# Tokens stationary in the second layer, weights split by bit operations, exponentials slot by slot for the first pairs

## The chip, the cores and the metric

The kernel runs on one core of a Trainium2 chip. It has five engines with a queue each: TensorE (matmuls; PE in the profile, PEld for its weight loads), VectorE (DVE), ScalarE (ACT), GpSimd (POOL) and SyncE (SP), which issues most transfers. An engine takes its instructions in order. The metric is device time in microseconds, the median of three runs.

## The reference

Eight batches of local attention feed a feed-forward block with a gate. All tensors are float32; the block's three weights are drawn as float64 and enter with 64 bits.

```python
# B, H, S, D = 8, 8, 576, 64; d_model 512, d_ff 1024
scores = q @ k.T / sqrt(D)
mask_plain = (rel >= 0) & (rel < 32)                       # heads 0 to 3
mask_dil = (rel >= 0) & (rel < 128) & (rel % 4 == 0)       # heads 4 to 7
attn = exp(scores - max); attn = attn / (sum(attn) + 1e-9)
x = (attn @ v), heads joined: (B, S, 512)
h = maximum(x @ w_in, 0)                                   # (B, S, 1024)
conv_out = conv_w[0]*h[s-1] + conv_w[1]*h[s] + conv_w[2]*h[s+1]
out = (h / (1 + exp(-conv_out))) @ w_out                   # (B, S, 512)
```

## The kernel before

**Precision.** Matmuls of the two layers take a cheap 32-bit type (`F32R`). Each operand is split into a rounded part and its remainder (`a` and `b`, or index 0 and 1), and a product is three matmuls (`TERMS`): part by part, part by remainder, remainder by part.

**Attention.** Heads go in pairs; a batch has pairs 0 and 1 (plain) and 2 and 3 (dilated). A pair's 576 queries lie in nine slots of 64 keys for 128 partitions. Its steps: 76 to 80 small matmuls of scores into the PSUM tile `att` (L248), mask added by VectorE (L254, L257), largest value of each slot (L260), subtraction (L262), exponential on ScalarE (L264), sum (L266), 1e-9 added (L268), reciprocal (L270), product (L271), transpose (L273), 96 small matmuls with the values into `att` (L283). ScalarE copies the result to `x` rounded (L320); the remainder is a subtraction on VectorE (L335), or, in batches 0 and 1, matmuls with minus the unit matrix on TensorE (L327, L330) and a second pair of ScalarE copies (L333). There is one `att`, so scores and values of all pairs take turns in it.

**First layer.** 128 hidden features (a chunk, eight of them) by 288 tokens (a half) are twelve matmuls (L353) into a PSUM tile `mm`, or `nn` for every second chunk of batch 0; there are two of each. ReLU goes to `h` on ScalarE (L360). `h` has three buffers, each with a whole chunk. Gating of a chunk: middle tap on ScalarE (L371), two taps on VectorE (L365), sigmoid (L376), product with `h` on VectorE (L378), which frees `h`; rounded part `g` on ScalarE (L380), remainder on VectorE (L382). `c`, the working tile, has three buffers, `g` one set of eight chunks.

**Second layer.** 128 output features by 288 tokens are 24 matmuls (L395): a 128x128 piece of `wo` is stationary and `g` moves. ScalarE copies out of PSUM (L402); a store goes out feature by feature, and the host turns the result.

**Weights.** A chunk of 512 words per partition comes in 64-bit form, two 32-bit words a value. ScalarE (L428) and VectorE (L430 to L441) build the rounded float32 and the rest. For the first ten of sixteen chunks TensorE adds them and takes off the rounded part (L450 to L452: a float32 matmul and two of `F32R`, 512 columns each), and ScalarE copies the remainder (L455). For six chunks VectorE does it (L457, L463).

**Order.** Every step is a task with an engine, a cost, a due time and buffers. `Planner.order` plays them through; on each engine, of the tasks that could start soon, the one with the earliest due time is taken. So the due times set the order, which is fixed when the program is built.

## Time and profile before

| | us |
|---|---|
| median of three runs (549.78 to 550.69) | 549.82 |
| span of the profiled execution, first to last instruction | 549.1 |
| TensorE busy | 522.4 |
| VectorE busy | 415.7 |
| ScalarE busy | 298.1 |
| mean granted TensorE clock, of full speed | 0.990 |

The profiled execution's span is 0.7 us below the median of the runs; the rest lies around it. "Busy" counts overlapping instructions once. A window row gives its length, then for an engine its busy time and, in brackets, instructions. Chain rows give start, length, engine, tile and line. Group rows give line, engine, operation, output<-input with shapes and count, then busy time and mean ns, then idle time ahead and what ended it.

### The profile page before, as it was taken

To read this page: it belongs to the slowest core of one execution; us is meant where nothing else is said; L and a number is where in the kernel's file an instruction comes from. 1 tells how busy PE (TensorE), PEld (TensorE's weight loads), DVE (VectorE), ACT (ScalarE), POOL (GpSimd) and SP (SyncE) were. 2 spreads that over 40 slices of the span, in tenths; PEclk is the share of its full clock that TensorE was granted. 3 is DMA by queue.
4 is the path that set the end of the run, shared out by engine and by line. 5 is a ranking of instruction groups with operands and counts; after the bars stand their busy time and mean duration, and the time that the engine had idled before them with its cause. 6 is when DMAs were issued, how large, how long until landed. Compare 5 with 4: busy or idle time off the path is not lost.

```text
span 549.1 us, 19084 instructions
## 1 busy us (share of the span) xinstructions
PE 522.4 (95%) x8664; PEld 497.2 (91%) x8664; DVE 415.7 (76%) x695; ACT 298.1 (54%) x556; POOL 0.9 (0%) x12
## 2 busy tenths in 40 slices
PE   3499978999999999999999999999999999999997
PEld 2468876999999999999999999999989999999997
DVE  4968998899997389946998389946988389946920
ACT  2457784855752486337742486237742486337721
POOL 0000000000000000000000000000000000000000
PEclk9999996999999999999999999999999999999999
DMA  7756513331044102630055102530045102300011
GB/s 247 268 157 215 195 52 137 119 121 44 7 138 152 30 23 65 200 110 23 13 161 170 32 23 72 190 113 23 17 152 162 45 23 58 117 26 23 0 44 44
DMA packets 17072, 52.31 MB, mean 95 GB/s; under 512 B 2016, under 2 KB 3168, under 8 KB 16992
## 3 DMA queue, kind: packets, MB, share of 16 engines
...
q10 hardware_dynamic: 144, 0.08, 0.1%
q14 instruction: 12, 0.10, 0.1%
...
## 4 chain that ended last, share of the span: by engine, by line
PE 92%; DVE 3%; ACT 2%; DMA 2%; issue 1%; ACTq 0%
PE nn L395 38%; PE mm L353 35%; PE att L283 8%; PE att L248 6%; PE nn L450 2%; PE nn L353 2%; PE att L327 1%; DMA qk<-in_qk_d_dram 1%; DMA qk<-in_qk_p_dram 1%; PE nn L451 0%; PE nn L452 0%; DVE pt L273 0%; DVE s L271 0%; PE att L330 0%; DVE c L365 0%
## 5 line engine op out<-in xcount | busy, mean ns | idle before, releaser
L365 DVE SCALAR_TENSOR_TENSOR c<-h,conv_sb,c 128x576 f32<-128x576 f32 x128 | 103.9, 815 | 48.4 <-ACT c L371 46.9
L360 ACT ACTIVATE h<-mm 128x288 f32<-128x288 f32 x120 | 48.8, 408 | 50.4 <-PE mm L353 50.1
L402 ACT COPY out<-nn 128x288 f32<-128x288 f32 x64 | 25.5, 400 | 70.1 <-PE nn L395 66.1
L378 DVE TENSOR_TENSOR c<-c,h 128x576 f32<-128x576 f32 x64 | 47.6, 755 | 9.4 <-ACT c L376 7.8
L283 PEld LDWEIGHTS att<-pt,v 32*64 32x64 f32 x3072 | 40.8, 138 | 14.8 <-DVE s L257 4.6
L283 PE MATMUL att<-pt,v 32*64 32x64 f32 (+2 forms) x3072 | 44.2, 232 | 9.4 <-DVE s L257 3.5
L371 ACT ACTIVATE c<-h,conv_sb 128x576 f32<-128x576 f32 x64 | 49.7, 776 | 1.3
L248 PE MATMUL att<-qk 64*32 64x64 f32 x2432 | 36.2, 235 | 11.0 <-DMA qk<-in_qk_d_dram 5.5
L248 PEld LDWEIGHTS att<-qk 64*32 64x32 f32 x2432 | 30.2, 111 | 16.9 <-DMA qk<-in_qk_d_dram 5.5
L376 ACT ACTIVATE c<-c 128x576 f32<-128x576 f32 x64 | 42.5, 678 | 2.1 <-DVE c L365 1.6
L353 PE MATMUL mm<-x2a,wi 128*128 128x288 f32 x144 | 40.5, 296 | 0.0
L353 PE MATMUL mm<-x1a,wi 128*128 128x288 f32 x144 | 40.3, 296 | 0.0
L353 PE MATMUL mm<-x3a,wi 128*128 128x288 f32 x144 | 40.3, 295 | 0.0
L353 PE MATMUL mm<-x0a,wi 128*128 128x288 f32 x144 | 40.3, 295 | 0.0
L395 PE MATMUL nn<-g2a,wo 128*128 128x288 f32 x128 | 37.0, 304 | 0.0
L395 PE MATMUL nn<-g0a,wo 128*128 128x288 f32 x128 | 36.4, 299 | 0.2
L395 PE MATMUL nn<-g6a,wo 128*128 128x288 f32 x128 | 36.6, 299 | 0.0
L395 PE MATMUL nn<-g3a,wo 128*128 128x288 f32 x128 | 36.4, 299 | 0.0
L395 PE MATMUL nn<-g1a,wo 128*128 128x288 f32 x128 | 36.4, 299 | 0.0
L395 PE MATMUL nn<-g4a,wo 128*128 128x288 f32 x128 | 36.4, 299 | 0.0
L395 PE MATMUL nn<-g5a,wo 128*128 128x288 f32 x128 | 36.4, 299 | 0.0
L395 PE MATMUL nn<-g7a,wo 128*128 128x288 f32 x128 | 36.1, 300 | 0.1
...
## 6 DMA issues: line engine op xcount, KB each, us to landing
...
out_dram<-out SPq DMA_DIRECT2D x28, 288.0 KB, 2.2
...
out<-in_w_in_dram SPq DMA_DIRECT2D x8, 512.0 KB, 4.5
out<-in_w_out_dram SPq DMA_DIRECT2D x8, 512.0 KB, 4.2
out_dram<-out SPq DMA_DIRECT2D x8, 144.0 KB, 1.8
```

Of the source, the lines that this page charges most:

```text
L248: nc.tensor.matmul(sc.t[quad * 32:quad * 32 + 32, slot // 4, slot % 4 * W:slot % 4 * W + W], q, k, start=i == 0, stop=i == len(parts) - 1, ...
L283: nc.tensor.matmul(tv.t[hd * 64:hd * 64 + 64, bank, o:o + n], v.t[quad * 32:quad * 32 + 32, block // 2, block % 2 * 64:block % 2 * 64 + 64 ...
L327: nc.tensor.matmul(tv.t[:, t, 0:128], minus, main[:, t], start=False, stop=True, skip_group_check=True)
L353: nc.tensor.matmul(ps.t[:, 0:HALF], wi[jw][fc][:, k * 128:k * 128 + 128], x[k].t[jx][:, hf * HALF:hf * HALF + HALF], start=(k == 0 and i = ...
L360: relu.append(plan.add("ACT", 0.4, due + 1.6 * u + 1.6, lambda fc=fc, hf=hf, ps=ps: nc.scalar.activation(out=h[fc].t[:, 1 + hf * HALF:1 + ...
L365: nc.vector.scalar_tensor_tensor(out=c[fc].t, in0=h[fc].t[:, k:S + k], scalar=conv_sb[:, k, fc:fc + 1], in1=c[fc].t, op0=ALU.mult, op1=ALU ...
L371: t = plan.add("ACT", 0.777, d, lambda fc=fc: nc.scalar.activation(out=c[fc].t, in_=h[fc].t[:, 1:S + 1], func=AF.Copy, scale=conv_sb[:, 1, ...
L376: t = plan.add("ACT", 0.686, d + 1.0, lambda fc=fc: nc.scalar.activation(out=c[fc].t, in_=c[fc].t, func=AF.Sigmoid), [t], [c[fc]], "sigmoid")
L378: t = plan.add("DVE", 0.755, d + 1.5, lambda fc=fc: nc.vector.tensor_tensor(out=c[fc].t, in0=c[fc].t, in1=h[fc].t[:, 1:S + 1], op=ALU.mult ...
L395: nc.tensor.matmul(ps.t[:, 0:HALF], wo[jw][2 * dm + k // 4][:, k % 4 * 128:k % 4 * 128 + 128], g[k].t[jg][:, hf * HALF:hf * HALF + HALF], ...
L402: outs.append(plan.add("ACT", 0.4, out_due + 3.3 + 3.3 * u, lambda hf=hf, ps=ps, o=o: nc.scalar.copy(out=o.t[:, hf * HALF:hf * HALF + HALF ...
L450: nc.tensor.matmul(ps.t, ident, t(), start=True, stop=False)
```

## The change

1. **Second layer.** Tokens become stationary (128 columns of `g`) and `wo` moves with 512 output features: 24 matmuls a job (L431) and one copy of 128x512 (L441). Batch 0 does two halves of 256 instead, since the halves of `wo` come one after the other. The output is stored token by token, and the host does not turn it.
2. **`g` for two batches.** 576 tokens are four and a half times 128. A `g` tile now holds two chunks, both parts, and 640 tokens: an even batch writes columns 0 to 575, the odd batch after it 64 to 639. An even batch does four jobs from column 64; the odd one five, the first with 64 tokens of each batch. A chunk of the odd batch is written when the even batch's jobs have read it (`done`).
3. **Weights.** Two chunks of 512 are converted together (1024 words), eight times. The rounded part is now cut by a mask in the second step (0x3ffff000), and the remainder is put together from the low word by a shift, a shift with an or, a mask and one product (L504 to L510). Nothing of it is on TensorE, and the ten sums are gone. The 24 convolution weights have their own short path (`few_weights`).
4. **Softmax.** For the first eight pairs (`SLOTS`: batches 0 and 1) ScalarE does nine exponentials, one a slot, with the negated largest value as bias and the sum as second output (L279); VectorE does no subtraction and no sum, and ScalarE scales the bias and adds the 1e-9 (L275, L283). The other pairs have a 65th column with 1e-9 in `s` that the sum takes in.
5. **Dilated copies.** `x` is written in order and `att` read in steps, where before read in order and wrote in steps.
6. **Order.** The due times are a new table, `DUE`, one for each task or series of tasks; `out` has two buffers instead of three.

```diff
+GW = S + 64
+PAIRED = 1024
+SLOTS, HELPED = 0xff, 0xff
+DUE = {
+    "first": (72.60, 66.90, 228.40, 589.20, 119.60, 531.50, -87.70, 234.00),
...
-    slots("s", 3, [128, 9, W])
+    ss = slots("s", 3, [128, 9, W + 1])
-    slots("g", NF, [128, S], F32R, 2)
+    slots("g", NF // 2, [128, 2, 2, GW], F32R)
-    slots("out", 3, [128, 1024])
-    slots("w", 2, [128, 512], F32, 2)
-    slots("r", 2, [128, 512], F32R)
+    slots("out", 2, [128, DM])
+    slots("raw", 2, [128, 2 * PAIRED], I32)
+    slots("t", 1, [128, PAIRED])
...
+        last = plan.add("DVE", 0.755, soft + 0.5, lambda: nc.vector.tensor_reduce(
+            out=m.t, in_=flat(), axis=AX.X, op=ALU.max, negate=slotwise), [last], [s, m])
+        if slotwise:
+            last = plan.add("ACT", 0.23, soft + 1.0, lambda: nc.scalar.mul(out=m.t, in_=m.t, mul=SCALE), [last], [m])
+            def exps():
+                for i in range(9):
+                    nc.scalar.activation(out=s.t[:, i, 0:W], in_=s.t[:, i, 0:W], func=AF.Exp, bias=m.t[:, i:i + 1],
+                                         scale=SCALE, accum_out=z.t[:, i:i + 1])
+            last = plan.add("ACT", 2.7, soft + 1.5, exps, [last], [s, m, z], "exp")
+            last = plan.add("ACT", 0.23, soft + 2.1, lambda: nc.scalar.add(out=z.t, in_=z.t, add=1e-9), [last], [z])
...
+            hi = plan.add("ACT", 0.675, d + 2.0, lambda fc=fc: nc.scalar.copy(out=half(fc, 0), in_=c[fc].t),
+                          [t, *(done[fc] if odd else [])], [c[fc], g[fc // 2]])
...
+        begins = [64 + 64 * odd + 128 * j for j in range(4)]
+        if odd:
+            begins = [0] + begins
+        jobs = [(c0, hf) for hf in range(2) for c0 in begins] if b == 0 else [(c0, None) for c0 in begins]
...
+                    nc.tensor.matmul(ps.t[:, 0:n], g[k // 2].t[:, k % 2, jg, c0:c0 + 128],
+                                     w.rearrange("p h c -> p (h c)") if hf is None else w[:, hf],
+                                     start=(k == 0 and i == 0), stop=(k == NF - 1 and i == 2))
...
+        last = plan.add("ACT", 1.14, due, lambda: nc.scalar.activation(out=t(), in_=hw(), func=AF.Abs), [load], [raw, tb])
+        last = step(0.69, [last], lambda: nc.vector.tensor_scalar(
+            out=t(), in0=t(), scalar1=2.0 ** -15, scalar2=None, op0=ALU.max))
+        last = step(0.69, [last], lambda: nc.vector.tensor_scalar(
+            out=bits(t), in0=bits(t), scalar1=3, scalar2=0x3ffff000,
+            op0=ALU.logical_shift_left, op1=ALU.bitwise_and))
+        top = step(1.22, [last], lambda: nc.vector.scalar_tensor_tensor(
+            out=bits(t), in0=bits(hw), scalar=-0x40000000, in1=bits(t), op0=ALU.bitwise_and, op1=ALU.bitwise_or))
+        high = plan.add("ACT", 1.14, due, lambda: nc.scalar.copy(out=hi, in_=shaped(t(), hi)), [top], [tb])
+        left = step(0.69, [load], lambda: nc.vector.tensor_scalar(
+            out=bits(lw), in0=bits(lw), scalar1=9, scalar2=None, op0=ALU.logical_shift_right))
+        left = step(1.22, [left], lambda: nc.vector.scalar_tensor_tensor(
+            out=bits(lw), in0=bits(hw), scalar=23, in1=bits(lw), op0=ALU.logical_shift_left, op1=ALU.bitwise_or))
+        last = step(0.69, [top, left], lambda: nc.vector.tensor_scalar(
+            out=bits(hw), in0=bits(t), scalar1=-0x800000, scalar2=None, op0=ALU.bitwise_and))
+        return [high, plan.add("DVE", 1.22, due, lambda: nc.vector.scalar_tensor_tensor(
+            out=lo, in0=shaped(lw().bitcast(U32), lo), scalar=2.0 ** -43, in1=shaped(hw(), lo),
+            op0=ALU.mult, op1=ALU.mult), [last], [raw])]
```

`lw` and `hw` are the low and high words of a value, every second word of `raw`.

Three places in the order of the built programs. Numbers behind an underscore tell buffers apart; `pt` is the transposed tile, `v` the values.

TensorE, near the start, before: a correction, the second value block, then the first weight sum.

```order
L327 MATMUL att_159<-x0a,minus 128x128 x4
L330 MATMUL att_159<-x0a,minus 128x32 x2
L283 MATMUL att_159<-pt_113,v_101 64x32 x8
L283 MATMUL att_159<-pt_113,v_101 64x64 x24
L283 MATMUL att_159<-pt_113,v_101 64x32 x16
L450 MATMUL nn_162<-w0b,ident 128x512
L451 MATMUL nn_162<-r_157,minus 128x512
L452 MATMUL nn_162<-wi_66,minus 128x512
```

The same place now: the value blocks of all four pairs of batch 0 follow one another, and then the first layer begins.

```order
L306 MATMUL att_124<-pt_94,v_81 64x32 x8
L306 MATMUL att_124<-pt_94,v_81 64x64 x24
L306 MATMUL att_124<-pt_94,v_81 64x32 x16
L351 MATMUL att_124<-x2a,minus 128x128 x4
L354 MATMUL att_124<-x2a,minus 128x32 x2
L306 MATMUL att_124<-pt_93,v_83 64x32 x8
L306 MATMUL att_124<-pt_93,v_83 64x64 x24
L306 MATMUL att_124<-pt_93,v_83 64x32 x16
L386 MATMUL mm_125<-x2a,wi_64 128x288
L386 MATMUL mm_125<-x2b,wi_64 128x288
```

The sums between the value blocks are gone, and the first layer begins four value blocks in, where before began after three.

VectorE, the gating of batch 0's first three chunks, before (`r` is the rest of a weight chunk).

```order
L378 TENSOR_TENSOR c_147<-c_147,h_144 128x576
L378 TENSOR_TENSOR c_148<-c_148,h_145 128x576
L365 SCALAR_TENSOR_TENSOR c_149<-h_146,conv_sb,c_149 128x576
L382 TENSOR_TENSOR g0b<-c_147,g0a 128x576
L254 TENSOR_TENSOR s_103<-att_159,mask_sb 128x512
L382 TENSOR_TENSOR g1b<-c_148,g1a 128x576
L257 TENSOR_TENSOR s_103<-att_159,mask_sb 128x64
L378 TENSOR_TENSOR c_149<-c_149,h_146 128x576
```

The same gating now; the last row is row 99 of VectorE's order.

```order
L411 TENSOR_TENSOR c_116<-c_116,h_113 128x576
L504 TENSOR_SCALAR raw_121<-raw_121 128x1024
L411 TENSOR_TENSOR c_117<-c_117,h_114 128x576
L415 TENSOR_TENSOR g_109<-c_116,g_109 128x576
L496 TENSOR_SCALAR t_123<-t_123 128x1024
L506 SCALAR_TENSOR_TENSOR raw_121<-raw_121 128x1024
L415 TENSOR_TENSOR g_109<-c_117,g_109 128x576
L411 TENSOR_TENSOR c_118<-c_118,h_115 128x576
```

Steps of batch 1's softmax stood between the gating steps (s_103); now those of all eight pairs lie ahead of it, and the first pair of output weight chunks (raw_121) stands there instead.

TensorE, second layer, before, in batch 3.

```order
L395 MATMUL nn_162<-g1a,wo_86 128x288
L395 MATMUL nn_162<-g1b,wo_86 128x288
L395 MATMUL nn_162<-g1a,wo_94 128x288
L395 MATMUL nn_162<-g2a,wo_86 128x288
L395 MATMUL nn_162<-g2b,wo_86 128x288
```

And now, in batch 1; `x2` stands for the two matmuls with the rounded part of `wo`.

```order
L431 MATMUL nn_127<-wo_73,g_111 128x512 x2
L431 MATMUL nn_127<-wo_75,g_111 128x512
L431 MATMUL nn_127<-wo_73,g_112 128x512 x2
L431 MATMUL nn_127<-wo_75,g_112 128x512
L431 MATMUL nn_127<-wo_73,g_112 128x512 x2
L431 MATMUL nn_127<-wo_75,g_112 128x512
```

Three matmuls of 288 columns became three of 512, and `g` stands where the weights stood.

More of the change, by code (lines that the diff above doesn't have):

```diff
@@ L273, in attention @@
-        last = plan.add("DVE", 0.755, due + 4.5, lambda: nc.vector.transpose(out=pt.t, in_=flat()), [last], [s, pt])
+        flat = lambda: s.t[:, :, 0:W]
+        halves = lambda t: t.rearrange("p (h a) k -> p h a k", h=2)
+        scored = lambda: (sc.t[:, 0:2, 0:256].rearrange("p h (a k) -> p h a k", k=W), sc.t[:, 2, 0:W])
+        two = lambda t: (halves(t[:, 0:8]), t[:, 8])
+        masked = mask_sb[:, kind].rearrange("p (a k) -> p a k", k=W)
+        wide = lambda t: t.unsqueeze(2).to_broadcast([128, 9, W])
@@ L275, in values @@
+        last = plan.add("DVE", 0.215, soft + 2.2, lambda: nc.vector.reciprocal(out=z.t, in_=z.t), [last], [z])
+        last = plan.add("DVE", 0.755, soft + 2.3, lambda: nc.vector.tensor_tensor(
+            out=flat(), in0=flat(), in1=wide(z.t), op=ALU.mult), [last], [s, z])
+        last = plan.add("DVE", 0.775, soft + 3.0, lambda: nc.vector.transpose(
+            out=pt.t.rearrange("p (a k) -> p a k", k=W), in_=flat()), [last], [s, pt])
         def values():
@@ L332, in attention @@
-            last = plan.add("PE", (0.42, 0.6)[kind], due + 7.2, less, his, [tv, x], "E")
-            return [plan.add("ACT", cost, due + 7.5, lambda i=i: nc.scalar.copy(out=parts(x.t[1])[i], in_=src(i)),
-                             [last], [tv, x]) for i, cost in ((0, (0.62, 1.12)[kind]), (1, (0.25, 0.3)[kind]))]
-        return [plan.add("DVE", cost, due + 7.5, lambda i=i: nc.vector.tensor_tensor(
+                    nc.tensor.matmul(tv.t[:, g, 128:160], minus,
+                                     rest[:, g] if kind == 0 else rest[:, :, g].rearrange("c m r -> c r m"), start=False,
+                                     stop=True, skip_group_check=True)
@@ L336, in attention @@
+            last = plan.add("PE", 0.6, val + 1.2, less, his, [tv, x], "E")
+            return [plan.add("ACT", cost, val + 1.5, lambda i=i: nc.scalar.copy(out=parts(x.t[1])[i], in_=src(i)),
+                             [last], [tv, x]) for i, cost in pieces]
+        return [plan.add("DVE", cost + 0.06 * (1 - i), val + 1.5, lambda i=i: nc.vector.tensor_tensor(
             out=parts(x.t[1])[i], in0=src(i), in1=parts(x.t[0].bitcast(F32))[i], op=ALU.subtract), his, [tv, x])
-            for i, cost in ((0, (0.68, 1.0)[kind]), (1, (0.215, 0.25)[kind]))]
+            for i, cost in pieces]
@@ new lines, in few_weights, with step @@
+    def few_weights(src, due):
+        u, t = few
+        low, high = (few_raw[:, :, i] for i in range(2))
+        ui, ti = u.bitcast(I32), t.bitcast(I32)
+        def step(run, after, engine="DVE"):
+            return plan.add(engine, 0.2, due, run, [after])
+        last = plan.add("SP", 0.1, due - 2.0, lambda: nc.sync.dma_start(
+            out=few_raw, in_=src.bitcast(I32).rearrange("p (n t) -> p n t", t=2)))
+        last = step(lambda: nc.scalar.activation(out=u, in_=high.bitcast(F32), func=AF.Abs), last, "ACT")
+        last = step(lambda: nc.vector.tensor_scalar(out=u, in0=u, scalar1=2.0 ** -15, scalar2=None, op0=ALU.max), last)
+        last = step(lambda: nc.vector.tensor_scalar(
+            out=ti, in0=ui, scalar1=3, scalar2=0x3fffffff, op0=ALU.logical_shift_left, op1=ALU.bitwise_and), last)
+        last = step(lambda: nc.vector.scalar_tensor_tensor(
+            out=ti, in0=high, scalar=-0x40000000, in1=ti, op0=ALU.bitwise_and, op1=ALU.bitwise_or), last)
+        last = step(lambda: nc.vector.tensor_scalar(
+            out=ui, in0=ti, scalar1=-0x800000, scalar2=None, op0=ALU.bitwise_and), last)
+        last = step(lambda: nc.vector.scalar_tensor_tensor(
+            out=u, in0=low.bitcast(U32), scalar=2.0 ** -52, in1=u, op0=ALU.mult, op1=ALU.mult), last)
+        return step(lambda: nc.vector.tensor_tensor(
+            out=conv_sb.rearrange("p t c -> p (t c)"), in0=t, in1=u, op=ALU.add), last)
@@ new lines, in weights, with step @@
+    def weights(src, due, fetch, hi, lo):
+        raw, tb = Buffer("raw"), Buffer("t")
+        part = lambda i: raw.t.rearrange("p (n w) -> p n w", w=2)[:, :, i]
+        lw, hw = (lambda i=i: part(i).bitcast(F32) for i in range(2))
+        t = lambda: tb.t
+        shaped = lambda x, like: x.rearrange("p (a c) -> p a c", a=like.shape[1])
+        whole = lambda x: x.rearrange("p a b c -> p a (b c)") if len(x.shape) == 4 else x
+        hi, lo = whole(hi), whole(lo)
+        bits = lambda x: x().bitcast(I32)
+        load = plan.add("SP", 3.0, fetch, lambda: nc.sync.dma_start(
+            out=raw.t, in_=src.bitcast(I32)), uses=[raw])
+        def step(cost, after, run):
+            return plan.add("DVE", cost, due, run, after, [raw, tb])
+        last = plan.add("ACT", 1.14, due, lambda: nc.scalar.activation(out=t(), in_=hw(), func=AF.Abs), [load], [raw, tb])
[16 more added lines that the diff above has]
+            op0=ALU.mult, op1=ALU.mult), [last], [raw])]
@@ L565 @@
     got = r.results[0]["out_0_dram"]
[L566 removed]
+    return got.reshape(B, S, DM)
```

235 lines of the change are left out of this document (99 added, 136 removed).

## The prediction

> **What bounds the kernel now.** I read the page's first line, then busy time in long stretches, then the chain of work that ended last.
>
> ```profile
> span 549.1 us, 19084 instructions
> ...
> 0.00:96.28 96.28, 74.44 (x1654) 0.95 0.52 181
> 96.28:545.60 449.32, 448.00 (x7012) 1.00 0.24 77
> ...
> 5.60:96.28 90.68, 80.89 (x158) 0.94 0.52 179
> ```
>
> The first two stretches are TensorE alone, the third VectorE alone (length, busy, granted clock, DMA share, GB/s). There are two regimes. Until 96.28, TensorE idles 22 us while VectorE works 81 of its first 91 us: VectorE bounds the start. From 96.28, where the second layer goes on behind batch 1's last value block, TensorE is busy 448.0 of 449.3 us at full clock: there only TensorE work counts, and time saved on VectorE or ScalarE is hidden by it. The last 3.5 us follow the last matmul.
>
> ```profile
> 28.11 2.00 PE nn L450 x2
> 53.08 0.86 PE nn L450 x2
> 53.94 0.23 PE nn L451
> 54.18 0.23 PE nn L452
> 92.30 1.84 PE nn L450 x2
> ...
> 35.74 0.99 PE mm L353 x6
> 96.28 1.78 PE nn L395 x12
> 114.61 19.09 PE nn L395 x144
> 244.11 7.94 PE mm L353 x60
> 254.85 16.30 PE mm L353 x123
> 305.80 7.94 PE mm L353 x60
> ...
> 80.00:82.00 2.00, 0.01 (x3) 1.00 0.00 0
> ```
>
> Pieces of the chain (start, length) first: a weight sum (L450 to L452) is 1.32 us of it at full clock, and the ten from 28.11 to 92.30, some at half clock behind idle time (2.00 for 0.86), are 18.4 us. 144 matmuls of 288 columns take 19.09 and 123 take 16.30, 132.5 ns each in either layer. One batch later the same place returns after 61.69 us; 384 matmuls are 50.9 of it, so four attention pairs cost TensorE 10.8, **2.7 us a pair**. The last row shows a hole in the start: TensorE still for two us.
>
> **Second layer.** 1536 matmuls of 288 columns, 203.5 us, become 192 of 256 (batch 0) and 768 of 512. The weight sums hold a matmul of the same type with 512 columns:
>
> ```profile
> 49.91 0.39 PE L452 MATMUL nn<-wi,minus 128*128 128x512 f32 x1
> 50.14 0.29 PE L353 MATMUL mm<-x1a,wi 128*128 128x288 f32 x1
> ```
>
> From its start to the next matmul's it is 0.23 us, as in the chain's pieces above. I take 230 ns, and 118.6 for 256 columns, on the line through 288 and 512. That is 768 x 0.230 + 192 x 0.1186 = 176.6 + 22.8 = 199.4: **-4.1 us**. The bounds: at 0.225, the least that two decimals allow, -7.9; in proportion to the columns (235.6 ns), about 0.
>
> Here a rule speaks for much more. The Trainium skill, "TensorE: Matmul & The Clock Gate", section "Back-to-back issue gap", gives about 131 ns a matmul at 512 columns for a sustained stream of loads and matmuls. By it the 768 would be 100.6 us, 76.0 less than by the row. The trace disagrees: 0.23 here, and already 132.5 ns with 288 columns in 19-us streams.
>
> **The start.** It gets its own sum, since VectorE decides it. The ten weight sums (three matmuls each) go from TensorE; VectorE converts 1024 words at a time, and for the first eight pairs it loses the subtraction (L262), the sum (L266) and the 1e-9 (L268).
>
> ```profile
> L254 DVE TENSOR_TENSOR s<-att,mask_sb 128x512 f32<-128x512 f32 x32 | 21.8, 680 | 2.4 <-PE att L248 2.3
> L257 DVE TENSOR_TENSOR s<-att,mask_sb 128x64 f32<-128x64 f32 x32 | 6.6, 208 | 0.0
> L260 DVE TENSOR_REDUCE m<-s 128x9 f32<-128x576 f32 x32 | 24.0, 751 | 0.8
> L270 DVE RECIPROCAL z<-z 128x9 f32<-128x9 f32 x32 | 6.9, 215 | 1.0
> L271 DVE TENSOR_TENSOR s<-s,z 128x576 f32<-128x576 f32 x32 | 24.2, 758 | 1.0
> L273 DVE STREAM_TRANSPOSE pt<-s 128x576 f32<-128x576 f32 x32 | 24.8, 776 | 0.9
> ...
> L365 DVE SCALAR_TENSOR_TENSOR c<-h,conv_sb,c 128x576 f32<-128x576 f32 x128 | 103.9, 815 | 48.4 <-ACT c L371 46.9
> L378 DVE TENSOR_TENSOR c<-c,h 128x576 f32<-128x576 f32 x64 | 47.6, 755 | 9.4 <-ACT c L376 7.8
> ...
> L430 DVE TENSOR_SCALAR w0a<-w0a 128x512 f32<-128x512 f32 x8 | 3.4, 422 | 2.6 <-ACT w0a L428 2.6
> L435 DVE SCALAR_TENSOR_TENSOR w0b<-out,w0b 128x512 int32<-128x512 int32 x8 | 5.5, 686 | 0.1
> L435 DVE SCALAR_TENSOR_TENSOR w0b<-out,w0b 128x24 int32<-128x24 int32 x1 | 0.2, 184 | 0.0
> L430 DVE TENSOR_SCALAR w0a<-w0a 128x24 f32<-128x24 f32 x1 | 0.2, 179 | 1.0 <-ACT w0a L428 1.0
> ...
> 5.64 0.45 DVE L472 COPY mask_sb<-kinds_sb 128x576 bf16<-128x576 bf16 x1 [5.64 <-DMA kinds_sb<-in_mask_dram]
> ...
> 75.29 0.76 DVE L382 TENSOR_TENSOR g3b<-c,g3a 128x576 fp32r<-128x576 f32 x1
> ```
>
> These are groups (busy, mean ns | idle before, releaser) and two single instructions (start, length). By the 24- and 512-wide rows, 1024 words cost 0.677 for one source and 1.213 for two; a converted pair of chunks is four of the first and three of the second, 6.35 us; before, two chunks with sums on TensorE were 2 x (3 x 0.422 + 2 x 0.686) = 5.28.
>
> TensorE stops in the new start where batch 0's chunk 7 needs the PSUM tile of chunk 5. ReLU must first empty that tile into an h buffer, which is free when VectorE has multiplied chunk 2 (new L411, row 99 of the new VectorE order). Up to this row stand eight pairs at 3.388 (27.1), four converted pairs of chunks (25.4), the first three steps of a fifth (2.57), six taps, three products and two remainders (8.7), masks and convolution weights (2.5): 66.2 us. How fast VectorE passes such rows shows in before: up to g3b 7.10 + 10.5 + 13.3 of attention, 22.2 of weights, 8.15 + 6.05 of gating and 1.45 of masks, 68.7 us, took 76.05 - 5.64 = 70.4. So row 99 ends at 5.64 + 66.2 x 70.4/68.7 = 73.5. Behind it stand two ReLUs (about 1.5 with a copy between them), 12 matmuls (1.6), the last value block (1.3), and its correction, which waits on TensorE between two pairs of ScalarE copies (about 4 by the x copies below): TensorE goes on at **82**, where before did at 96.28: **-14.3 us**. On its own TensorE would be there sooner: first L386 at about 39 (before 35.74; a fifth score block and the nine exponentials of pair five are queued ahead of the copies that it needs), 25.4 for 192 matmuls and about 11 for three score blocks, four value blocks and corrections, 76. The 18.4 us of sums and the hole at 80 are therefore not gained in full; VectorE takes the place of both.
>
> What VectorE and ScalarE lose behind the start lies beside the busy TensorE and counts as nothing; were TensorE idle there, it would be worth its length. ScalarE's new work in the start, the copies and the moved transfers are costed by these rows:
>
> ```profile
> L320 ACT CAST x0a<-att 128x64 fp32r<-128x64 f32 x5 | 1.2, 249 | 10.3 <-PE att L283 8.4 <-DVE s L271 1.9
> L333 ACT CAST x3b<-att 128x512 fp32r<-128x512 f32 x1 | 1.1, 1094 | 0.0
> L333 ACT CAST x2b<-att 128x512 fp32r<-128x512 f32 x1 | 0.6, 585 | 0.4 <-PE att L330 0.4
> ...
> L402 ACT COPY out<-nn 128x288 f32<-128x288 f32 x64 | 25.5, 400 | 70.1 <-PE nn L395 66.1 <-issue 1.4 <-DVE w1a L441 1.4
> L455 ACT CAST wi<-nn 128x512 fp32r<-128x512 f32 x8 | 4.7, 584 | 6.1 <-PE nn L452 6.0
> ...
> out_dram<-out SPq DMA_DIRECT2D x28, 288.0 KB, 2.2
> out_dram<-out SPq DMA_DIRECT2D x8, 144.0 KB, 1.8
> out<-in_w_in_dram SPq DMA_DIRECT2D x8, 512.0 KB, 4.5
> ```
>
> No row has an exponential of 64 with an accumulated sum; the bounds are 0.25 (L320) and 0.40 (L402), 2.2 or 3.6 us for nine. I take 0.27, near the row of the same width; ScalarE is idle enough to hide it, and the upper end would delay the start by about 4. The dilated copies now write in order and read PSUM in steps: 0.585 (contiguous pair) to 1.094 (dilated, stepped writes); I take 0.6. The first fetch of 1 MB stands fourth in SP's queue, ahead of the third pair's queries; at twice 4.5 us it lands at about 11, and VectorE wants it at row 18, about 12: nothing, and what it is later VectorE waits. The eight 1-MB fetches and the stores of 256 KB are issued in place of sixteen and 28 of like bytes and are hidden as those are.
>
> **The sum**, against the profiled execution's 549.1: start -14.3; second layer -4.1; batch 1's first chunks wait for h at 82 (a chunk takes 3.2 on TensorE and 3.14 of taps, product and remainder on VectorE, with weights between them), **+2.0**; end, a copy of 0.584 for 0.400 and a store between 1.8 and 2.2 where 1.8 stood, **+0.5**. First layer, 2.7 us a pair and before's few waits stay. 549.1 - 15.9 = 533.2. The median run is 549.82, 0.7 above the span: **534**.
>
> **The rivals.** *Strided words at full price (541 to 547).* Two of the four one-source steps now write every second word (L504, L508). The trace has one-source steps on contiguous words only, 0.422 for 512 against 0.686 with two sources. If a stride loses that, 16 steps cost 0.54 more each: 4.9 us ahead of row 99, 8.7 in all, since the second layer waits for the last chunk; with 0.6 to 3 us for dilated copies at 1.094 where only nine matmuls (2.07) part two value blocks, 543 to 546. The Trainium skill, "VectorE: DVE Perf Modes", section "What auto-detection actually checks", has the fast mode depend on a single source and on both ends lying in SBUF, not on the step, and no run here shows a stepped one; this speaks against the rival.
>
> *TensorE sets the start (522 to 527).* If ReLUs come sooner, it goes on at 76 and nothing waits behind: -8, and with 225 ns -4 more.
>
> *Columns overlap (458).* If 512 columns cost 131 ns, 76 us go. The L452 rows speak against it.
>
> *Slower: one set of g (556).* g has one set for two batches, handed out two chunks at a time. If at each of seven batch changes a chunk's VectorE rows (1.63 + 0.755 + 0.76 = 3.14) came to stand between the layers, 22 us would be added. It decides against the change from 15.9/7 = 2.3 us a change. Against it: before has one set too and TensorE is busy 448.0 of 449.3; the last job of a batch now lasts 24 x 0.23 = 5.5 us instead of 3.2, so the first g comes free earlier ahead of its end.
>
> *The sums go and nothing is gained (549).* That needs the start at 96 again, 14 us of VectorE more than its rows add up to.
>
> **How the numbers follow.** Forecast 0.62 (527 to 541); strided words, slow copies or slow exponentials 0.18 (541 to 547); early start 0.10 (522 to 527); columns 0.02; no gain 0.03; slower 0.05. The range 522 to 546 holds the first three but for a little. A measurement here tells about 0.2% from no change: faster 0.92, same 0.03, slower 0.05.
>
> **What would show it.** L431's 512 columns start 225 to 235 ns apart; one-source steps on 1024 words take 0.68; row 99 ends near 73.5 and the first matmul of batch 1's first layer starts near 82; TensorE is busy over 98% from about 125 on; L279 takes 0.25 to 0.3. A TensorE hole of over 2 us at each batch change, or a start beyond 90, would make the forecast wrong.

## The result and the profile after

The changed kernel takes **535.58 us** (median of four runs, 535.31 to 536.71), the kernel before beside it 549.80: a ratio of 0.9743, 95% interval 0.9729 to 0.9757. The forecast was 534.0, range 522 to 546. The profiled execution has a span of 533.8 where before had 549.1, so 15.3 us are to be found; the prediction's sum had 15.9.

First the page of the changed kernel, its lines on the span and on TensorE, and the chain's shares by engine.

```profile
span 533.8 us, 17819 instructions
...
PE 505.9 (95%) x8048; PEld 449.4 (84%) x8048; DVE 397.3 (74%) x611; ACT 303.7 (57%) x660; POOL 1.0 (0%) x15
...
PE 80%; DVE 8%; ACT 7%; DMA 3%; issue 1%; ACTq 0%
```

Then the stretches of time: from, to, length, then busy us and instructions of PE, PEld, DVE, ACT, POOL, the granted clock, DMA share and GB/s. The changed kernel:

```profile
0.00:41.00 41.00, 20.52 (x779) 18.06 (x780) 31.17 (x58) 27.95 (x121) 1.01 (x15) 1.00 0.70 250
76.00:85.00 9.00, 9.00 (x155) 8.77 (x154) 8.72 (x13) 7.78 (x18) 0.00 (x0) 1.00 0.16 47
85.00:92.00 7.00, 6.97 (x52) 6.62 (x51) 6.78 (x10) 6.34 (x13) 0.00 (x0) 1.00 0.00 0
85.00:134.00 49.00, 48.25 (x513) 46.41 (x512) 46.01 (x60) 32.52 (x55) 0.00 (x0) 1.00 0.26 89
```

The kernel before, at the place where the two part:

```profile
76.00:85.00 9.00, 5.24 (x124) 4.90 (x122) 8.69 (x19) 6.03 (x11) 0.00 (x0) 0.93 0.07 20
85.00:92.00 7.00, 6.21 (x109) 4.84 (x108) 6.83 (x13) 3.43 (x7) 0.00 (x0) 0.50 0.46 164
92.00:97.00 5.00, 5.00 (x111) 3.71 (x111) 3.46 (x6) 3.15 (x6) 0.00 (x0) 0.81 0.32 113
97.00:110.00 13.00, 13.00 (x165) 12.74 (x164) 10.78 (x20) 10.64 (x18) 0.00 (x0) 1.00 0.38 124
```

Between 76 and 92 TensorE of the kernel before has holes, and then works at a granted clock of 0.50, the lower of its two levels (1.2 of 2.4 GHz); in the changed kernel it has none, at 1.00. A busy share says little about how far TensorE has come, though, since ends of matmuls are modelled. So I counted matmuls. These rows are the stretch from 0 to 100 for one line each (busy us and count of matmuls, then of weight loads): before, first layer, scores, values,

```profile
0.00:100.00 100.00, 28.17 (x192) 26.16 (x192) 0.95 0.52 178
0.00:100.00 100.00, 10.43 (x608) 8.61 (x608) 0.95 0.52 178
0.00:100.00 100.00, 12.49 (x768) 11.62 (x768) 0.95 0.52 178
```

and the changed kernel, in the same order:

```profile
0.00:100.00 100.00, 43.67 (x288) 40.11 (x289) 1.00 0.53 184
0.00:100.00 100.00, 11.22 (x608) 9.08 (x608) 1.00 0.53 184
0.00:100.00 100.00, 13.08 (x768) 12.21 (x768) 1.00 0.53 184
```

Attention stands alike at 100, and of the second layer 26 and 24 matmuls are done; the changed kernel is 96 first-layer matmuls ahead, 12.7 us at 0.1324. Counted so at several times, with 0.1324 us for 288 columns, 0.2334 for 512, 0.118 for 256, 1.25 for a block of scores and 1.45 for one of values (2.7 a pair; weight sums and corrections not counted), the clock minus the work done is **the time that TensorE has lost so far**, whatever the profile calls busy. It is worked out, not read; the columns of three experiments are used further on.

| at | before | changed | sums cut | whole exps | w_out twice |
|---|---|---|---|---|---|
| 41 | 29.0 | 28.9 | 29.0 | 30.5 | 28.6 |
| 60 | 33.8 | 32.7 | 33.2 | 35.1 | 32.0 |
| 76 | 36.1 | 35.9 | 35.8 | 41.1 | 35.3 |
| 85 | 40.9 | 36.7 | 40.9 | 42.7 | 36.0 |
| 100 | 49.5 | 37.4 | 51.0 | 44.0 | 38.1 |
| 134 | 49.5 | 37.8 | 51.4 | 43.8 | 41.4 |
| 400 | 50.0 | 37.4 | 53.2 | 44.0 | 41.7 |

Up to 76 the two kernels are level. Then before loses 13.4 us and the changed one 1.5; from 100 to their last matmuls it is 3.0 and 0.7. What before does there is shown by TensorE's timeline (start, length, and in brackets the idle time ahead with what ended it):

```profile
81.98 1.26 PE L283 MATMUL att<-pt,v 32*64 32x32 f32 x96 [2.97 <-DVE pt L273]
84.03 1.12 PE L327 MATMUL att<-x5a,minus 128*128 128x128 f32 x4 [0.79 <-ACT x5a L320]
...
86.29 2.06 PE L283 MATMUL att<-pt,v 32*64 32x64 f32 x96 [0.79 <-ACT x5b L333]
88.28 2.08 PE L450 MATMUL nn<-w0b,ident 128*128 128x512 f32 x2
```

Batch 0's first layer is done at 79.0, its second waits for VectorE to convert the output weights, and what is left to TensorE is three value blocks in one PSUM tile, the first two behind softmax and behind the copies of the one before, and two weight sums (88.28 to 91.00 and 92.14 to 94.44). The sums are 5.0 of the 13.4 us, idle time from 76 to 92 is 4.6; the rest is the low clock and the corrections. In the changed kernel the value blocks lie between first-layer matmuls, and batch 1's first layer follows at once:

```profile
82.97 0.68 PE L351 MATMUL att<-x2a,minus 128*128 128x128 f32 x4
83.47 0.31 PE L354 MATMUL att<-x2a,minus 128*128 128x32 f32 x2
83.64 0.38 PE L386 MATMUL mm<-x6a,wi 128*128 128x288 f32 x1
```

The account of the 15.3 us: to their last matmuls (545.6 and 529.8) the two have lost 52.5 and 38.1, a difference of 14.4; the second layer costs 1.5 less (below); the end costs 0.5 more, a copy and a store as forecast (3.5 us behind the last matmul before, 4.0 now).

The operations of the change, by groups (busy, mean ns | idle before):

```profile
L506 DVE SCALAR_TENSOR_TENSOR raw<-raw 128x1024 int32<-128x1024 int32 x8 | 9.8, 1225 | 0.1
L508 DVE TENSOR_SCALAR raw<-t 128x1024 int32<-128x1024 int32 x8 | 5.5, 693 | 0.2
L496 DVE TENSOR_SCALAR t<-t 128x1024 f32<-128x1024 f32 x8 | 5.5, 682 | 0.0
...
L279 ACT ACTIVATE s<-s,m 128x64 f32<-128x64 f32 x72 | 24.0, 340 | 0.2
L279 ACT ACTIVATION_READ_ACCUMULATOR s<-s,m 128x1 f32 x72 | 13.7, 191 | 0.0
...
L344 ACT CAST x2a<-att 128x512 fp32r<-128x512 f32 x5 | 3.0, 591 | 0.0
```

Strided words cost next to nothing extra (L508 steps, L496 does not: 693 and 682 ns), the dilated copies came out at the lower bound (591), and each exponential has a second instruction behind it.

Pieces of the chain of the changed kernel (start, length, what):

```profile
9.37 3.10 ACT s L279 x18
...
211.91 5.09 DMA qk<-in_qk_p_dram
...
265.54 11.20 PE nn L431 x48
...
502.44 27.32 PE nn L431 x117
```

Nine exponentials take 3.10 us. 48 and 117 matmuls of 512 columns start some 233.4 ns apart. And the chain puts 5.09 us on a late query fetch; that one is a trap. The timeline of TensorE in that stretch:

```profile
211.81 5.17 PE L431 MATMUL nn<-wo,g 128*128 128x512 f32 x21
217.13 0.96 PE L258 MATMUL att<-qk 64*32 64x64 f32 x72 [0.16 <-DMA qk<-in_qk_p_dram]
```

TensorE did 21 matmuls meanwhile; the fetch cost 0.16.

### The profile page after: what moved, and what is told of

Its sections match the earlier page's. It is cut to its first block, busy times and chain, and to the rows that moved or that the text cites. A ratio compares the mean times of both kernels' runs of the same rounds, so it can differ in the third digit from the quotient of the medians.

```text
span 533.8 us, 17819 instructions
## 1 busy us (share of the span) xinstructions
PE 505.9 (95%) x8048; PEld 449.4 (84%) x8048; DVE 397.3 (74%) x611; ACT 303.7 (57%) x660; POOL 1.0 (0%) x15
## 3 DMA queue, kind: packets, MB, share of 16 engines
q1 hardware_dynamic: 16336, 51.02, 28.6%
## 4 chain that ended last, share of the span: by engine, by line
PE 80%; DVE 8%; ACT 7%; DMA 3%; issue 1%; ACTq 0%
PE nn L431 34%; PE mm L386 31%; PE att L306 8%; PE att L258 4%; ACT s L279 3%; PE nn L386 2%; DVE c L398 2%; PE att L351 1%; DMA qk<-in_qk_p_dram 1%; DVE t L501 1%; DVE wo L510 1%; ACT c L409 1%; DMA c<-in_mask_dram 1%; DVE c L411 1%; DVE g L415 1%
## 5 line engine op out<-in xcount | busy, mean ns | idle before, releaser
L431 PE MATMUL nn<-wo,g 128*128 128x512 f32 (+1 forms) x960 | 212.0, 375 | 0.0
L431 PEld LDWEIGHTS nn<-wo,g 128*128 128x128 f32 x960 | 163.4, 188 | 33.4
L393 ACT ACTIVATE h<-mm 128x288 f32<-128x288 f32 x120 | 48.5, 408 | 43.9 <-PE mm L386 40.8
L441 ACT COPY out<-nn 128x512 f32<-128x512 f32 (+1 forms) x40 | 21.7, 542 | 72.5 <-PE nn L431 45.1
L413 ACT CAST g<-c 128x576 fp32r<-128x576 f32 x64 | 42.4, 672 | 17.7 <-DVE c L411 15.7
L415 DVE TENSOR_TENSOR g<-c,g 128x576 fp32r<-128x576 f32 x64 | 47.6, 755 | 4.5 <-ACT g L413 3.4
L258 PE MATMUL att<-qk 64*32 64x64 f32 x2432 | 36.6, 237 | 13.4 <-DMA qk<-in_qk_p_dram 5.3
L270 DVE TENSOR_TENSOR s<-att,mask_sb 128x512 f32<-128x512 f32 x64 | 26.6, 450 | 16.3 <-PE att L258 16.2
L386 PE MATMUL mm<-x6a,wi 128*128 128x288 f32 x128 | 36.6, 301 | 0.8 <-ACT h L393 0.7
L386 PE MATMUL mm<-x5a,wi 128*128 128x288 f32 x128 | 36.2, 298 | 0.2 <-ACT h L393 0.2
L386 PE MATMUL mm<-x4a,wi 128*128 128x288 f32 x128 | 35.9, 295 | 0.0
L295 DVE STREAM_TRANSPOSE pt<-s 128x576 f32<-128x576 f32 x32 | 24.8, 776 | 11.9 <-PE att L306 10.9
```

The lines of the kernel that those rows point to most:

```text
L258: nc.tensor.matmul(sc.t[quad * 32:quad * 32 + 32, slot // 4, slot % 4 * W:slot % 4 * W + W], q, k, start=i == 0, stop=i == len(parts) - 1, ...
L270: last = plan.add("DVE", cost, soft + 0.0, lambda i=i: nc.vector.tensor_tensor(out=two(flat())[i], in0=scored()[i], in1=two(masked)[i], op ...
L386: nc.tensor.matmul(ps.t[:, 0:HALF], wi[jw][fc // 2][:, fc % 2, k], x[k].t[jx][:, hf * HALF:hf * HALF + HALF], start=(k == 0 and i == 0), s ...
L393: relu.append(plan.add("ACT", 0.4, due + 1.6 * u + 1.6, lambda fc=fc, hf=hf, ps=ps: nc.scalar.activation(out=h[fc].t[:, 1 + hf * HALF:1 + ...
L413: hi = plan.add("ACT", 0.675, d + 2.0, lambda fc=fc: nc.scalar.copy(out=half(fc, 0), in_=c[fc].t), [t, *(done[fc] if odd else [])], [c[fc] ...
L415: lo = plan.add("DVE", 0.755, d + 2.5, lambda fc=fc: nc.vector.tensor_tensor(out=half(fc, 1), in0=c[fc].t, in1=half(fc, 0).bitcast(F32), o ...
```

## The experiments

Differences between single runs of one kernel reach 4 us here, so below some 2 us the median decides little, and the profile's events are read beside it. All ratios are to the kernel before on the same chip; the changed kernel's is 0.9743. In the kernels built from the changed one the order on every engine is the changed kernel's, unless said otherwise.

### The sums alone, taken out of the kernel before

```diff
-                nc.tensor.matmul(ps.t, ident, t(), start=True, stop=False)
-                nc.tensor.matmul(ps.t, minus, r.t, start=False, stop=False)
-                nc.tensor.matmul(ps.t, minus, hi, start=False, stop=True)
+                nc.tensor.matmul(ps.t, minus, r.t, start=True, stop=True)
```

> The kernel before with two of the three matmuls of each of the ten weight sums on TensorE left out (those with the identity and with the rounded half; the low halves of the weights come out wrong): about 10 x (0.86 + 0.23) = 10.9 us of TensorE work less, VectorE's and ScalarE's rows unchanged. Theory A, the sums lay on the path, as the 18.4 us of the chain say: 8 to 15 us shorter, 535 to 542. Theory B, VectorE bounds that start and the sums filled its waits: 0 to 3 us shorter, 547 to 550; then the gain of the change comes from VectorE's rows, not from the sums.

Of each sum the matmul with `r` stays; gone are 30 of 40, which are 15.7 of the chain's 18.4 us. 552.58 us, ratio 1.005 (1.0033 to 1.0067): 3 longer than the 549.55 beside it, where no theory had longer. Theory A falls; B is right that the sums filled waits, but not in its number. The hole is longer, and the stretches behind it show a lower clock:

```profile
83.27 1.87 PE L283 MATMUL att<-pt,v 32*64 32x32 f32 x96 [4.47 <-DVE pt L273]
...
85.00:92.00 7.00, 4.86 (x110) 4.08 (x106) 6.79 (x15) 3.66 (x9) 0.00 (x0) 0.50 0.29 85
92.00:97.00 5.00, 5.00 (x108) 4.53 (x109) 4.89 (x7) 3.31 (x7) 0.00 (x0) 0.50 0.69 258
97.00:110.00 13.00, 13.00 (x153) 12.74 (x153) 8.79 (x15) 10.29 (x17) 0.00 (x0) 0.87 0.38 122
```

The first value block of the three comes 1.3 us later (83.27 for 81.98), because VectorE's transpose does. TensorE works less between 85 and 92 (4.86 for 6.21) and stays at the lower clock longer: 0.50 from 92 to 97 and 0.87 to 110, where before had 0.81 and 1.00. The lost time is 51.0 at 100 for 49.5, and 53.2 at 400 for 50.0. How the 3 us divide between the later block and the clock is not shown. The matmuls that the chain charged with 15.7 us were worth less than nothing.

### The exponentials whole again

```diff
-            out=m.t, in_=flat(), axis=AX.X, op=ALU.max, negate=slotwise), [last], [s, m])
+        def maxima():
+            nc.vector.tensor_reduce(out=m.t, in_=flat(), axis=AX.X, op=ALU.max)
+            if slotwise:
+                nc.vector.tensor_tensor(out=flat(), in0=flat(), in1=wide(m.t), op=ALU.subtract)
...
-                for i in range(9):
-                    nc.scalar.activation(out=s.t[:, i, 0:W], in_=s.t[:, i, 0:W], func=AF.Exp, bias=m.t[:, i:i + 1],
-                                         scale=SCALE, accum_out=z.t[:, i:i + 1])
+                nc.scalar.activation(out=flat(), in_=flat(), func=AF.Exp, scale=SCALE)
...
```

> The changed kernel with the exponentials of the first eight pairs in one instruction again: VectorE subtracts the maxima and adds up the sums (2 x 0.75 a pair, 12 us in all), ScalarE has one exponential of 0.69 in place of nine and two small ones (about 2.8 us a pair less, 22 in all); all else stands in the same order. Theory A, ScalarE's blocks of 3.10 us are what the first 41 us wait for and VectorE has room: -2 to +2 us, 533.5 to 537.5. Theory B, the prediction's, VectorE's rows up to row 99 set the start: 66.2 + 12 us of rows instead of 66.2, +10 to +12 us, 545.5 to 547.5.

541.78 us, 0.9849 (0.9825 to 0.9873): 6.2 longer than the changed kernel, between the theories. On VectorE the row that ended at 76.2 in the changed kernel (row 99) ends later; the timelines, first of the changed kernel,

```profile
75.45 0.75 DVE L411 TENSOR_TENSOR c<-c,h 128x576 f32<-128x576 f32 x1
```

then with whole exponentials:

```profile
82.40 0.75 DVE L419 TENSOR_TENSOR c<-c,h 128x576 f32<-128x576 f32 x1
```

6.95 us for 12 us of rows: the rest went into VectorE's idle time (in the changed kernel 9.8 us of the first 41). The lost time at 400 is 44.0 for 37.4. So the part "slot by slot" is worth some 6 of the 15 us, and it is worth them through VectorE.

### The accumulated sums left out

```diff
-                                         scale=SCALE, accum_out=z.t[:, i:i + 1])
+                                         scale=SCALE)
...
-            last = plan.add("ACT", 0.23, soft + 2.1, lambda: nc.scalar.add(out=z.t, in_=z.t, add=1e-9), [last], [z])
+            last = plan.add("ACT", 0.23, soft + 2.1, lambda: nc.scalar.add(out=z.t, in_=m.t, add=1e-9), [last], [z])
```

> The changed kernel with the nine exponentials of each of the first eight pairs without their accumulated sum; the rows are then divided by their maximum in place of their sum, and everything stands in the same order on every engine. In the changed kernel nine exponentials take 3.10 us (0.33 a slot, with a second instruction of 0.19 behind each). Theory A, ScalarE's exponentials set the first 41 us (four blocks in a row from 9.37 to 23.95, the fifth ahead of the copies of the third pair): a block falls to about 2.3 us, the first value block comes about 3 us sooner than 22.51, and the time is 3 to 4.5 us shorter, 531 to 532.5. Theory B, the rows of VectorE set the start, as the prediction had it: less than 1 us, 534.6 to 535.6.

534.16 us, 0.9721 (0.9703 to 0.9739), span 532.2: 1.4 to 1.6 less, between the two theories; the interval overlaps the changed kernel's. The block became as short as expected, and the gain did not follow. ScalarE's and TensorE's timelines of this kernel:

```profile
9.18 2.26 ACT L279 ACTIVATE s<-s,m 128x64 f32<-128x64 f32 x9
```

```profile
21.87 2.06 PE L306 MATMUL att<-pt,v 32*64 32x64 f32 x96 [0.95 <-DVE s L270]
...
38.88 0.61 PE L386 MATMUL mm<-x2a,wi 128*128 128x288 f32 x1
```

2.26 for 3.10, so the read costs 0.093 us a slot on ScalarE. But the first value block came only 0.64 sooner (21.87 for 22.51), behind the same row of VectorE that it waits for in the changed kernel; the first layer came 1.9 sooner (38.88 for 40.81).

### TensorE and VectorE cut in the start, one by one and together

TensorE (24 matmuls):

```diff
                 for i, (jw, jx) in enumerate(TERMS):
+                    if b == 0 and fc > 3 and k and jw:
+                        continue
...
```

> The changed kernel with 24 matmuls of batch 0's first layer left out (the third term for chunks 4 to 7, for all k but the first), 24 x 0.1325 = 3.2 us of TensorE work at the end of the start; nothing else moves. Theory A, TensorE sets the start from 41 on by its own work: 2.5 to 3.2 us shorter, 532.4 to 533.1. Theory B, the prediction's, the ReLUs behind VectorE's row 99 hold TensorE there: under 0.5 us, 535.1 to 535.6.

VectorE (four rows; `less` is true for two of the eight pairs of chunks):

```diff
-        left = step(0.69, [load], lambda: nc.vector.tensor_scalar(
+        left = step(0.69, [load], lambda: None if less else nc.vector.tensor_scalar(
...
-        left = step(1.22, [left], lambda: nc.vector.scalar_tensor_tensor(
+        left = step(1.22, [left], lambda: None if less else nc.vector.scalar_tensor_tensor(
```

> The changed kernel with two of VectorE's steps (shift of the low words, low words with the high words' bits) left out for the fourth pair of chunks of w_in and the first of w_out: 2 x (0.69 + 1.22) = 3.8 us of VectorE work ahead of row 99, all in the stretch 50 to 75. Theory A, TensorE sets the start: 0 to 0.7 us shorter, 534.9 to 535.6, though row 99 ends 2 us or more sooner than 76.2. Theory B, VectorE's rows set it: 3 to 3.8 us shorter, 531.8 to 532.6.

> The changed kernel with both cuts at once: 24 matmuls of batch 0's first layer left out (3.2 us of TensorE) and two of VectorE's steps for two pairs of chunks (3.8 us). Each alone gave 533 to 537 in single runs, no change. Theory A, the end of the start is set by two limits that lie within a microsecond of each other, TensorE's own work and the rows of VectorE that free h: only the two cuts together shorten it, by 2 to 3.2 us, 532.4 to 533.6. Theory B, a third thing sets it (fetches, ScalarE's queue): no change, 535 to 536.

534.46 us (532.83 to 536.76, 0.9728, 0.9696 to 0.9761) without the matmuls, 535.43 (533.27 to 535.88, 0.9735, 0.9709 to 0.9761) without the rows, 534.14 (532.50 to 535.49, 0.9714, 0.9682 to 0.9745) without both. By the times alone neither cut is told from no change, and only the pair leans towards shorter; it gave two runs near 532.8 (one of them the profiled one, span 531.3, 2.5 below the changed kernel's) and two near 535.4, so theory A is possible and not shown.

The profiles say more. Without the matmuls TensorE stands idle longer between 41 and 85 (4.0 us for 2.0), so part of the cut came back as waits:

```profile
41.00:85.00 44.00, 40.02 (x827) 37.03 (x823) 38.39 (x55) 36.17 (x115) 0.00 (x0) 1.00 0.49 163
```

Without the four VectorE rows the row 99 ended no sooner (76.85), against both theories, because VectorE then waits more for TensorE and ScalarE: 7.7 us between 41 and 77, where it was 3.5. Pieces of its timeline:

```profile
72.57 0.76 DVE L411 TENSOR_TENSOR c<-c,h 128x576 f32<-128x576 f32 x1 [0.52 <-ACT c L409]
...
76.09 0.76 DVE L411 TENSOR_TENSOR c<-c,h 128x576 f32<-128x576 f32 x1
```

Neither engine is the bound of the changed kernel's start by itself. Taking from one of them gives little or nothing, putting on VectorE costs (the whole exponentials), and the next run shows the same behind the start.

### The last step for w_out done twice

```diff
-        return [high, plan.add("DVE", 1.22, due, lambda: nc.vector.scalar_tensor_tensor(
-            out=lo, in0=shaped(lw().bitcast(U32), lo), scalar=2.0 ** -43, in1=shaped(hw(), lo),
-            op0=ALU.mult, op1=ALU.mult), [last], [raw])]
+        def rest():
+            for _ in range(2 if twice else 1):
+                nc.vector.scalar_tensor_tensor(out=lo, in0=shaped(lw().bitcast(U32), lo), scalar=2.0 ** -43,
+                                               in1=shaped(hw(), lo), op0=ALU.mult, op1=ALU.mult)
...
```

> The changed kernel with VectorE's last step of each of the four pairs of chunks of w_out done twice: 4 x 1.23 = 4.9 us of VectorE work between 93 and 118. Theory A, TensorE works without a hole from 85 on (48.25 us busy of 49 between 85 and 134) and the chain's walk through VectorE there is a tie of equals: 0 to 0.7 us, 535.6 to 536.3. Theory B, the chain of waits is to be taken at its word between 84 and 133 and VectorE sets that stretch: 4 to 5 us longer, 539.6 to 540.6.

541.45 us (539.60 to 542.35), 0.9843 (0.9816 to 0.9871): theory B, and a little more. TensorE, which had no hole between 85 and 133, now has three, each in front of the second layer's matmuls that take the weights just made:

```profile
95.66 2.86 PE L431 MATMUL nn<-wo,g 128*128 128x256 f32 x22 [1.11 <-DVE wo L513]
108.27 11.34 PE L431 MATMUL nn<-wo,g 128*128 128x256 f32 x94 [1.17 <-DVE wo L513]
123.21 8.48 PE L431 MATMUL nn<-wo,g 128*128 128x256 f32 x70 [1.70 <-DVE wo L513]
```

1.11 + 1.17 + 1.70 = 3.98, the 4.0 that the profiled span grew by (537.8). So the chain's walk through VectorE from 84 to 133 is real, although TensorE shows no hole there: the weights come just as TensorE reaches for them. Both engines are full; VectorE has almost no slack. The lost time at 400 is 41.7 for 37.4.

### 512 columns cut into halves

```diff
-                    nc.tensor.matmul(ps.t[:, 0:n], g[k // 2].t[:, k % 2, jg, c0:c0 + 128],
+                    for q in ((0, 1) if hf is None else (hf,)):
+                        at = 256 * q if hf is None else 0
+                        nc.tensor.matmul(ps.t[:, at:at + 256], g[k // 2].t[:, k % 2, jg, c0:c0 + 128], w[:, q],
...
```

> The changed kernel with each of the 768 matmuls of 512 columns in batches 1 to 7 cut into two of 256 (the same work, the same order). In the changed kernel's chain 117 matmuls of 512 take 27.32 us, 233.5 ns each, and 24 of 256 take 2.94, 122.5 each. Theory A, a matmul costs a fixed part beside its columns (2 x 122.5 - 233.5 = 11.5 ns): 768 x 0.0115 = 8.8 us longer, 544.4. Theory B, the prediction's line through 288 and 512 columns (118.6 and 230): 768 x 0.0072 = 5.5 longer, 541. Theory C, in proportion to the columns: no change.

535.67 us (533.12 to 537.46), 0.9732 (0.9693 to 0.9771): no change, as theory C had it. A's 8.8 and B's 5.5 are refuted; A's 122.5 ns held the change-over from another kind of matmul. The profiled span, 535.7, is 1.9 above the changed kernel's, but it belongs to the slowest of four runs that differ by 4.3. Two long pieces of this kernel's chain:

```profile
268.16 11.31 PE nn L433 x96
...
505.15 26.55 PE nn L433 x234
```

That is 117.8 and 113.5 ns each: 256 columns do not always cost the same here, and why is open. Twice that is 235.6 and 227.0, on either side of the 233.4 for 512. The number of matmuls hardly counts; the columns do.

### Due times alone, in the kernel before

```diff
-    DUE = {0: (-9.2, 2.8, 30.4), 1: (64.7, 50.1, 92.3)}
-    PAIR = {0: (-26.0, -24.7, -23.0, -27.0), 1: (-4.9, 1.3, 8.9, 14.5)}
-    WI, WO = (-20.4, -20.4, -7.2, -7.2, -3.1, -0.1, 7.8, 7.8), (17.2, 17.2, 36.3, 36.3, 36.9, 34.9, 43.2, 43.2)
+    DUE = {0: (-9.2, 2.8, 60.4), 1: (20.7, 30.1, 92.3)}
+    PAIR = {0: (-26.0, -24.7, -23.0, -27.0), 1: (-14.9, -8.7, -5.1, 0.5)}
+    WI, WO = (-20.4, -20.4, -7.2, -7.2, -3.1, -0.1, 7.8, 7.8), (37.2, 37.2, 46.3, 46.3, 56.9, 54.9, 63.2, 63.2)
```

> The kernel before with other due times alone: batch 1's four pairs 10 us sooner, batch 1's first layer ahead of batch 0's second, the conversion of w_out some 20 us later, so that all eight value blocks stand between matmuls of batch 0's first layer and 168 matmuls of batch 1's first layer follow it, much as in the changed kernel; every operation is that of before. Before, TensorE's progress falls 13.4 us behind between 76 and 100, while the changed kernel loses 1.6 there. Theory A, the new order closes that gap, whatever the operations cost: 6 to 10 us shorter, 540 to 544. Theory B, the order alone is worth little, since VectorE's rows are as long as before and only end later: within 2 us of before, 548 to 551.

The second of the two leaves PAIR as it was:

> The kernel before with fewer due times moved: batch 1's first layer ahead of batch 0's second and w_out's conversion later, but batch 1's pairs as in before, so that the last three value blocks still stand one behind the other after batch 0's first layer (without the two weight sums that stood between them). Theory A, it is the second layer's wait for w_out that makes the gap: as much as with the pairs moved too, 6 to 10 us shorter. Theory B, the gap is the row of value blocks itself, which wait for softmax and for each other: 2 to 5 us shorter at most, 545 to 548. Theory C, the order is worth nothing: 549 to 551.

575.09 us (1.0451, 1.0413 to 1.0489) and 566.58 us (1.0288, 1.0263 to 1.0313): 25 and 16.5 longer, where no theory had longer. Each order made holes of its own. In the first, VectorE has little to do from 41 to 60; in the second, from 100 to 120. One row of each (length, then busy us of PE, PEld, DVE, ACT):

```profile
41.00:60.00 19.00, 19.00 (x415) 16.06 (x405) 8.21 (x20) 10.79 (x24) 0.00 (x0) 0.80 0.59 199
```

```profile
100.00:120.00 20.00, 20.00 (x132) 18.87 (x132) 10.20 (x16) 10.73 (x22) 0.00 (x0) 0.93 0.15 53
```

With 10 to 11 us of VectorE's time unused there, its rows end later. In the first, TensorE then waits 12.9 us for rows of the weights (L450 behind L435) and has a granted clock of 0.57 from 100 to 120. In the second its waits are shorter (3.5 at most behind VectorE's transpose), and it has a clock of 0.50 from 85 to 100, where before had 0.70; what makes up its 16.5 us is not worked out. These two orders are not the changed kernel's, so what the order is worth by itself stays open; that batch 1's first layer put ahead of batch 0's second is enough is refuted.

### Two attempts to go below the changed kernel

The low halves of batch 0's pairs by one subtraction on VectorE:

```diff
+            def rest(i):
+                if b == 0:
+                    for i in (0, 1) if i == 0 else ():
+                        nc.vector.tensor_tensor(out=parts(x.t[1])[i], in0=src(i), in1=parts(x.t[0].bitcast(F32))[i],
+                                                op=ALU.subtract)
+                else:
+                    nc.scalar.copy(out=parts(x.t[1])[i], in_=src(i))
...
-            last = plan.add("PE", 0.6, val + 1.2, less, his, [tv, x], "E")
+            last = plan.add("PE", 0.6, val + 1.2, less if b else lambda: None, his, [tv, x], "E")
...
```

> The changed kernel with the low halves of batch 0's four pairs made by one subtraction each on VectorE (0.70 + 0.22 us) in place of the correction on TensorE and its copies on ScalarE (about 1.1 + 0.4 + 0.7 us with the waits between them), in the chain from 22.5 to 42.4 where the four value blocks pass one PSUM tile in a row at 5.5 us each; all else stands in the same order. Theory A, that chain is what the start waits for: the first matmul of the first layer comes 2 to 4 us sooner than 40.88, and the time is 1 to 3 us shorter, 532.5 to 534.5. Theory B, TensorE and VectorE are both full from 41 on, and 3.7 us more on VectorE take back what the chain gains: 535 to 538.

534.66 us (533.33 to 535.47), 0.9705 (0.9682 to 0.9727): about 1 less by the medians, 2 by the ratios, whose intervals just miss each other (0.9727, 0.9729); it lies between the theories. The first layer began at 39.98 instead of 40.81, less than expected, since the fourth value block waited 4.16 for x2b:

```profile
38.20 1.85 PE L306 MATMUL att<-pt,v 32*64 32x32 f32 x96 [4.16 <-DVE x2b L361]
39.98 0.61 PE L393 MATMUL mm<-x2a,wi 128*128 128x288 f32 x1
```

So in the last run that wait was attacked:

```diff
-        for t in plan.order():
+        order = [t for t in plan.order() if t not in moved]
+        at = max(order.index(t) for t in copied) + 1
+        order[at:at] = moved
+        for t in order:
```

(`copied` are the third pair's two copies, `moved` its subtraction and the fifth pair's exponentials.)

> The changed kernel with batch 0's low halves on VectorE (as in the run before this) and, besides, the third pair's copies and its subtraction put ahead of the fifth pair's nine exponentials and of the rows that wait for these; there the fourth value block stood 4.2 us waiting for x2b. Theory A, the row of four value blocks is what the start waits for: the first matmul of the first layer starts 1 to 2 us sooner than 39.98, and the time is 1 to 2.5 us below the changed kernel's, 533 to 534.6. Theory B, TensorE and VectorE, both full from 41 on, take it back: 535 to 536.5.

536.45 us (535.42 to 538.22), 0.9763 (0.9744 to 0.9782): theory B. The first layer began at 39.32, sooner still, and the next wait took its place: the sixth score block, which needs the same PSUM tile, stood 2.97 behind x3b, queued on VectorE behind rows of the weights.

```profile
39.32 0.61 PE L401 MATMUL mm<-x2a,wi 128*128 128x288 f32 x1
...
45.07 1.60 PE L259 MATMUL att<-qk 64*32 64x64 f32 x80 [2.97 <-DVE x3b L366]
```

## Why the prediction was right, step by step

**VectorE decides the start; TensorE goes on at 82 where before did at 96.28.** The place came out at 83.64, and at 100 the changed kernel has lost 12.1 us less, where -14.3 and +2.0 had 12.3; the 2.3 more by the end the forecast did not have. That the sums are not gained as such was right: cutting them alone gave nothing. That VectorE's rows carry the gain is shown from one side: giving back 12 us of them cost 6.2. But 82 was worked out through a wait that did not occur (next point), so that the place agrees within 2 us is in part luck.

**Row 99 at 73.5, and TensorE held behind it.** The row ended at 76.2, and this step of the mechanism failed: no hole stands behind it; TensorE runs through from 72 to 85. The rival "TensorE sets the start" had the mechanism half right (first matmul at 39, in fact at 40.81; then its own work), but not its 76: with 2 us of holes, twelve matmuls that start 0.24 us apart instead of 0.132 (40.8 to 45), and about 14 us of blocks and corrections instead of 11 (an estimate, what is left of the stretch), it was 83.64. What bounds the start is neither alone.

**The exponentials, 0.27 a slot.** Mis-sized: 3.10 / 9 = 0.344, towards the upper bound of 0.40. The price of the difference was given as up to 4 us; without the read of the sum, 0.25 a slot, 1.4 to 1.6 us came back, not clear of the spread of the runs.

**Second layer, 230 ns and 118.6 ns, -4.1 us.** The starts are 233.4 ns and 118 ns apart: 768 x 0.2334 + 192 x 0.118 = 201.9 for 203.4, **-1.5** (-2.4 at 113.5 for 256 columns). The term that was mis-sized is the 0.23 read from a column with two decimals; the bounds (-7.9 to about 0) held. Columns do not overlap: 512 take 233.4 ns. The 131 ns that the Trainium skill has for 512 columns ("TensorE: Matmul & The Clock Gate", section "Back-to-back issue gap") is not what this stream of 32-bit matmuls does.

**Strided words (0.18), slow copies.** Refuted: 693 ns against 682, and copies at 591. The Trainium skill ("VectorE: DVE Perf Modes", section "What auto-detection actually checks") names no step among the conditions of the two-port fast mode of a single source, and the rows agree: 693 and 682 ns.

**Slower, one set of g.** Not seen: TensorE's longest wait for an h buffer is 1.1 us, and the lost time stands at 37.4 at 100 and at 400.

**"What VectorE loses behind the start counts as nothing."** Wrong as a rule. Up to 123 VectorE's rows for w_out come just in time, and 4.9 us more cost 4.0 in the profile and 5.9 in the median. That the change's own rows just fit there, so that the number held, was luck.

**Waits of batch 1's first chunks +2.0, end +0.5.** The first are under 1 us (48.25 busy of 49 between 85 and 134); the end is as forecast.

**What each part is worth.** Of the 15.3 us, slot by slot is worth some 6 by experiment, and the second layer 1.5 to 2.4 by its starts. How the rest is shared between the order, the conversion and the missing sums is not shown.
